# A new written-out order for the first batch, and the next batch's product of keys one step later

## The chip, the cores and the metric

The kernel runs on one core of one Trainium2 chip. The metric is the device time of one launch in microseconds (us). A core has five engines that work side by side, each through its own instructions in the order in which they were written for it: TensorE (PE, matrix products; PEld is its weight load), VectorE (DVE), ScalarE (ACT), GpSimd (POOL) and SyncE (SP, here the queue that issues the DMA transfers). An instruction waits until what it reads is there and what it overwrites is free, and everything behind it on its engine waits with it.

## The reference

Three layers stand one behind the other. The weights of the second, `w_in` and `w_out`, come as 64-bit floats, which the kernel reads as pairs of 32-bit words.

```python
# attention: q, k, v [8, 8, 576, 64], phi [8, 8, 576, 32]
a = softmax(phi, axis=2)                       # over the 576 positions
k_m = einsum('bhsm,bhsd->bhmd', a, k)          # product of keys
v_m = einsum('bhsm,bhsd->bhmd', a, v)          # product of values
x = softmax(q @ k_m.T / 8) @ v_m               # [8, 8, 576, 64] -> 4608 x 512
# a layer with ELU: w_in 512 x 2048, w_out 2048 x 512 (64-bit floats)
h = x @ w_in
y = where(h > 0, h, exp(min(h, 0)) - 1) @ w_out
# one of eight experts per row: w1 512 x 1024, w2 1024 x 512
e = argmax(y @ w_gate); out = gate * relu(y @ w1[e]) @ w2[e]
```

## The kernel before, in words

**Steps.** A batch is 576 rows, taken as two groups `g` of 288 columns; the ELU layer's 2048 inner columns are 16 blocks `f`. One step `(b, g, f)` is `mm1` (6 matmuls on PE, L509), `elu` (ACT L516, L517, DVE L518), `split_g` (`gh`, ACT's cast L525, and the rest `gl = e - gh`, L526, on DVE or POOL) and `mm2` (12 matmuls, L541: for each of four accumulators `gh`, `gl`, and `gh` with the low part `wol` of the weights). Each fp32 product is split into a high and a low part in this way. There are 256 steps; the first 25, of batch 0 (its second group is begun first, 8 blocks, then the first group), have numbers in the order below (`mm1.23`, `g.23`).

**Conversion.** In the first batch the weights are also loaded and converted, as 16 slices `n` of 1024 KB (even: `w_in`, odd: `w_out`). `x.n` loads one (SP, L241 or L249), `A0.n` is on ACT (L264, L269), `A1.n` three instructions on DVE (L278, L281, L284), `R.n` one on POOL (L292). Four slices (`FINE`) are done in two halves. For `w_in` the slice is then multiplied with the values (`M.s` PE L471, `Me.s` ACT L480 and DVE L481) and written out (`B.n`); for `w_out` it is cast (`C.n`, ACT L308) and its low part formed (`D.n.u`, L320: 4 of the 16 on PE, 5 on DVE by `LO_V`, 7 on POOL). The sixteenth slice's `D.15.0` and `D.15.1` are the last, and step 23 (`mm2.23`, block 15) needs them.

**Attention.** For a batch and each half `u` of the heads: loads `phi.u` (288 KB), `kv.u` (2 x 576 KB), `q.u` (three pieces, 576 KB); `a1` to `a2` the first softmax; `a3` the product of keys and values (PE L369), `a3b` (DVE L379 to L388); `a4t` turns the queries over (DVE L400), `a4` the scores (PE L413); `a5` (DVE L423), `a5e` (POOL L428), `a5b`, `a5m` (POOL L441), `a5c` (DVE L446), `a5d` (ACT L458, POOL L459). A name with `n.` in front belongs to the next batch (1), whose attention is prepared in the first batch's last steps. Its keys and values go into the buffer in which the slices were converted (tag `kv`, one buffer), its queries into one of two buffers that slices also use (tag `big`). `w.k` loads a converted part of `w_in` again; `n.M.k` multiplies it with batch 1's values. `routing` sets the tables for the third layer up (POOL, a few small DVE casts, and a DMA that fills `itab`).

**Order.** `START` is a list of these names; the program calls them in that order, and so sets each engine's order by hand, up to step 23. `LATER` gives the names that come at the head of steps 24 and on. From step 24 a scheduler places the instructions. `GL_V` lists the steps among the first 25 whose `gl` is formed on DVE; the others' are formed on POOL.

Of the kernel before, what the change touches and what calls it, by code (L numbers as in the profile page):

```python
# [23 lines left out]


START = """
routing phi.0 R.2.1 A1.9.1 x.1 kv.0 a1.0 A1.2.1 phi.1 a1e.0 A0.1 a2.0.0 R.7.1 a2.0.1 A1.1.0 A1.1.1 R.1.1 R.1.0 a3.0
q.0 a1.1 a1e.1 a2.1.0 a3b.0 A1.8.1 R.5.1 a4t.0 x.2 kv.1 a2.1.1 A0.2 a4.0 C.1 q.1 a5.0 R.3.1 A1.7.1 x.3 A1.2.0 x.0
a5e.0 a5b.0 D.1.1 D.1.0 a5m.0 a4t.1 a3.1 R.2.0 x.5 a5c.0 a3b.1 a4.1 a5d.0 A1.3.1 a5.1 A0.3 A1.3.0 a3c A0.0 a5e.1
a5b.1 M.1 A1.0.0 R.3.0 R.0.1 A0.5 a5m.1 a5c.1 x.4 C.3 D.3.0 R.11.1 R.0.0 Me.1 A0.4 x.6 a5d.1 D.3.1 A1.4.0 B.2 M.0  # L30
Me.0 R.4.1 A1.5.0 mm1.0 A0.6 elu.0 mm1.2 A1.6.0 R.14.1 elu.2 R.4.0 g.0 A1.4.1 M.2 Me.2 mm1.1 R.5.0 elu.1 R.12.1 C.5
mm1.3 A1.6.1 B.4 elu.3 D.5.1 g.1 mm1.4 R.6.0 R.8.1 g.2 x.7 mm2.0 A0.7 A1.5.1 R.6.1 M.3 A1.7.0 elu.4 mm1.5 A1.15.1
D.5.0 A1.14.1 x.8 mm2.1 x.9 mm2.2 g.3 Me.3 elu.5 mm1.6 mm1.7 B.6 mm2.3 R.7.0 A0.8 g.4 elu.6 A1.8.0 mm1.8 A1.12.1
A1.11.1 elu.7 C.7 mm2.4 g.5 A0.9 mm1.9 g.7 g.6 A1.9.0 D.7.1 R.8.0 B.0 x.10 elu.8 D.7.0 B.8 A1.0.1 R.9.0 elu.9 A0.10
mm2.5 g.8 swap R.9.1 mm2.6 n.phi.0 A1.10.0 mm1.10 mm2.7 M.4 elu.10 R.15.1 C.9 g.9 x.11 x.12 part mm1.11 elu.11
R.10.0 mm1.12 mm2.8 A1.10.1 Me.4 mm1.13 mm2.9 elu.12 g.10 A0.11 D.9.0 D.9.1 A1.11.0 mm1.15 R.10.1 x.13 mm2.10 elu.13
M.5 mm1.14 g.11 g.12 mm2.11 A0.12 A1.12.0 mm2.12 R.11.0 g.13 B.10 mm2.13 elu.14 Me.5 elu.15 C.11 n.a1.0 g.14 R.12.0
D.11.0 mm1.17 A0.13 D.11.1 M.6 mm1.16 elu.17 mm2.14 A1.13.0 x.14 mm1.18 g.15 elu.16 g.17 mm2.15 A1.13.1 R.13.0 Me.6
elu.18 g.16 A0.14 mm1.19 A1.14.0 R.13.1 mm2.16 g.18 elu.19 B.12 x.15 A0.15 n.q.0 mm1.20 A1.15.0 R.14.0 C.13 mm2.17
mm2.18 g.19 w.0 elu.20 M.7 Me.7 mm1.21 elu.21 D.13.0 g.20 mm2.19 g.21 R.15.0 C.15 mm1.22 n.phi.1 D.13.1 mm2.20  # L40
D.15.1 elu.22 D.15.0 B.14 mm2.21 g.22 n.q.1 n.kv.0 n.a4t.0 n.a1e.0 w.1 mm2.22 n.a2.0 n.a1.1 mm1.24 mm1.23 n.a4t.1
elu.24 elu.23 g.24 g.23 n.a1e.1
"""
# [1239 lines left out]
```

## Time and profile before

| | us |
|---|---|
| median of 3 runs | 1393.47 |
| lowest and highest of them | 1391.57, 1393.93 |
| the profiled execution | 1395.19 |
| its span in the profile | 1393.5 |

The profile is that of one execution; its times count from the span's start. A wait stands in brackets behind the instruction that waited, with what released it. The page's busy shares are means over the whole span; the change touches its first seventh.

### The profile page before, as it was taken

To read this page: it belongs to the slowest core of one execution; us is meant where nothing else is said; L and a number is where in the kernel's file an instruction comes from. 1 tells how busy PE (TensorE), PEld (TensorE's weight loads), DVE (VectorE), ACT (ScalarE), POOL (GpSimd) and SP (SyncE) were. 2 spreads that over 40 slices of the span, in tenths; PEclk is the share of its full clock that TensorE was granted. 3 is DMA by queue.
4 is the path that set the end of the run, shared out by engine and by line. 5 is a ranking of instruction groups with operands and counts; after the bars stand their busy time and mean duration, and the time that the engine had idled before them with its cause. 6 is when DMAs were issued, how large, how long until landed. Compare 5 with 4: busy or idle time off the path is not lost. (4 is left out here: it accounts for less than half of the span.)

```text
span 1393.5 us, 27587 instructions
## 1 busy us (share of the span) xinstructions
PE 1299.6 (93%) x9407; PEld 1114.5 (80%) x9407; DVE 626.4 (45%) x1359; ACT 633.6 (45%) x1377; POOL 433.9 (31%) x476
## 2 busy tenths in 40 slices
PE   4497899999999999999999999999999999999996
PEld 2287688889889889799789899878888888888885
DVE  4899564434534434444443324654223555342221
ACT  3577455555555555555555646423112344231110
POOL 2555143433433434334344343221111111111111
PEclk9999999999999999999999999999999999999998
DMA  9766656324434433442521510063111444111010
GB/s 211 198 192 198 171 140 133 90 90 97 106 80 98 136 71 94 112 94 75 130 48 42 163 33 18 18 222 129 38 46 42 167 149 144 60 47 47 32 47 31
DMA packets 57626, 140.74 MB, mean 101 GB/s; under 512 B 9321, under 2 KB 21738, under 8 KB 53872
## 3 DMA queue, kind: packets, MB, share of 16 engines
q1 hardware_dynamic: 49328, 118.15, 31.4%
q0 software_dynamic: 8128, 20.50, 4.6%
q8 instruction: 85, 1.39, 0.5%
q14 instruction: 85, 0.70, 0.2%
HBM read 253.79 MB, written 24.02 MB: 199 GB/s over the span
## 5 line engine op out<-in xcount | busy, mean ns | idle before, releaser
L541 PE MATMUL ps_acc<-gl,wt 128*128 128x288 f32 x1024 | 305.7, 299 | 6.4 <-DVE gl L526 3.7
L526 POOL TENSOR_TENSOR gl<-e,gh 128x288 fp32r<-128x288 f32 x237 | 192.0, 812 | 382.2 <-ACT gh L525 296.7
L541 PE MATMUL ps_acc<-gh,wt 128*128 128x288 f32 x1024 | 304.4, 297 | 0.0
L541 PE MATMUL ps_acc<-gh,wol 128*128 128x288 f32 x1024 | 302.2, 295 | 0.0
L509 PE MATMUL ps_h<-ath,wt 128*128 128x288 f32 x1024 | 261.9, 311 | 16.4 <-DVE e L518 15.9
L509 PEld LDWEIGHTS ps_h<-ath,wt 128*128 128x128 f32 x1024 | 179.5, 189 | 58.2 <-issue 29.9
L518 DVE SCALAR_TENSOR_TENSOR e<-e,ps_h 128x288 f32<-128x288 f32 x256 | 115.1, 450 | 230.1 <-ACT e L517 200.7
L541 PEld LDWEIGHTS ps_acc<-gl,wt 128*128 128x128 f32 x1024 | 194.6, 190 | 11.3 <-POOL gl L526 5.6
L1109 PE MATMUL ps_h<-wt,xh 128*128 x592 | 195.1, 400 | 1.3 <-ACT xh L1090 0.8
L541 PEld LDWEIGHTS ps_acc<-gh,wt 128*128 128x128 f32 x1024 | 194.9, 190 | 0.6 <-issue 0.6
L541 PEld LDWEIGHTS ps_acc<-gh,wol 128*128 128x128 f32 x1024 | 194.3, 190 | 0.0
L525 ACT CAST gh<-e 128x288 fp32r<-128x288 f32 x256 | 109.9, 430 | 152.3 <-DVE e L518 150.4
L1150 POOL DMA_INDIRECT out_dram<-ot,idw x37 | 37.1, 1004 | 388.4 <-DVE ot L1149 376.6
L509 PE MATMUL ps_h<-atl,wt 128*128 128x288 f32 x512 | 152.4, 298 | 0.0
L516 ACT ACTIVATE e<-ps_h 128x288 f32<-128x288 f32 x256 | 105.0, 410 | 89.0 <-PE ps_h L509 71.4
L1109 PEld LDWEIGHTS ps_h<-wt,xh 128*128 128x128 f32 x592 | 111.4, 188 | 27.0 <-ACT xh L1090 1.0
L1143 PE MATMUL ps_acc<-wt1h,hh 128*128 x296 | 120.6, 407 | 5.6 <-PEq L1187 5.6
L1125 ACT CAST hh<-ps_acc 128x512 fp32r<-128x512 f32 x74 | 39.8, 590 | 175.6 <-PE ps_acc L1123 175.5
L1143 PE MATMUL ps_acc<-wt1l,hh 128*128 x296 | 118.4, 400 | 0.0
L1143 PE MATMUL ps_acc<-wt1h,hl 128*128 x296 | 117.7, 397 | 0.0
L1109 PE MATMUL ps_h<-wt,xl 128*128 x296 | 117.2, 396 | 0.2 <-DVE xl L1091 0.2
L517 ACT ACTIVATE e<-e 128x288 f32<-128x288 f32 x256 | 113.8, 444 | 7.2
(242 smaller groups left out, 1824.9 us busy)
## 6 DMA issues: line engine op xcount, KB each, us to landing
raw<-in_moe_w_dram SPq DMA_DIRECT2D x78, 2048.0 KB
win<-win_s SPq DMA_DIRECT2D x28, 1024.0 KB
kv<-in_k_dram SPq DMA_DIRECT2D x16, 576.0 KB
kv<-in_v_dram SPq DMA_DIRECT2D x16, 576.0 KB
table<-yr SPq DMA_DIRECT2D x144, 64.0 KB
big<-in_moe_w_out_dram SPq DMA_DIRECT2D x10, 512.0 KB
phi_t<-in_phi_dram SPq DMA_DIRECT2D x16, 288.0 KB
big<-in_q_dram SPq DMA_DIRECT2D x16, 288.0 KB
```

The source lines that it names most:

```text
L509: nc.tensor.matmul(ps, x[:, u, fo:fo + P], y[:, u], start=(n == 0), stop=(n == 3 * NQ - 1))
L516: nc.scalar.activation(out=e, in_=ps, func=AF.Relu, scale=-1.0)
L517: nc.scalar.activation(out=e, in_=e, func=AF.Exp, scale=-1.0)
L518: nc.vector.scalar_tensor_tensor(out=e, in0=e, scalar=-1.0, in1=ps, op0=ALU.add, op1=ALU.max)
L525: nc.scalar.copy(out=gh, in_=e)
L526: eng.tensor_tensor(out=gl, in0=e, in1=gh.bitcast(F32), op=ALU.subtract)
L541: nc.tensor.matmul(acc[c], x[:, f, P * c:P * c + P], y, start=(first and n == 0), stop=(final and n == 2),)
L1109: nc.tensor.matmul(ps, x[:, c], half(wt[0][y][2 * c + hf]), start=(i == 0), stop=(i == 3 * NC - 1))
L1125: nc.scalar.copy(out=h, in_=ps)
L1143: nc.tensor.matmul(ps, get(h, f), half(wt[1][y][f]), start=(i == 0), stop=(i == 3 * NF2 - 1))
L1150: nc.gpsimd.indirect_dma_start(out=out, out_offset=IndirectOffsetOnAxis(ap=at, axis=0), in_=ot, in_offset=None, bounds_check=NT - 1, oob_i ...
```

## The change

It writes another order for the first batch (`START`), moves one of the five `D` on DVE to another half (`LO_V`), forms five more `gl` of the first 25 on POOL (`GL_V` falls from 19 to 14), and sets the next batch's product of keys and what follows from it one step later (`LATER`).

```diff
--- before.py
+++ after.py
@@ -24,30 +24,30 @@
 START = """
-routing phi.0 R.2.1 A1.9.1 x.1 kv.0 a1.0 A1.2.1 phi.1 a1e.0 A0.1 a2.0.0 R.7.1 a2.0.1 A1.1.0 A1.1.1 R.1.1 R.1.0 a3.0
...
+R.2.1 phi.0 a1.0 kv.0 R.12.1 phi.1 a1e.0 R.5.1 A1.12.1 q.0 q.1 a2.0.0 a1.1 a2.0.1 R.3.1 a3.0 a3b.0 A1.8.1 kv.1 R.8.1
...
 """
 LATER = {
-    24: "n.a3.0 n.a3b.0 n.kv.1 n.a2.1",
-    25: "n.a4.0 n.a5.0 n.a5e.0",
-    26: "n.a3.1 n.a3b.1 n.a5b.0 n.a5m.0 n.q2.0",
-    27: "n.pk2 n.a3c n.a4.1 n.a5.1 n.a5e.1 n.a5c.0",
-    28: "n.M.0 n.a5b.1 n.a5m.1 n.q2.1",
-    29: "n.a5d.0 n.a5c.1 n.a5d.1",
+    25: "n.a3.0 n.a3b.0 n.kv.1 n.a2.1",
+    26: "n.a4.0 n.a5.0 n.a5e.0",
+    27: "n.a3.1 n.a3b.1 n.a5b.0 n.a5m.0 n.q2.0",
+    28: "n.pk2 n.a3c n.a4.1 n.a5.1 n.a5e.1 n.a5c.0 n.M.0",
+    29: "n.a5b.1 n.a5m.1 n.q2.1 n.a5d.0",
+    30: "n.a5c.1 n.a5d.1",
     31: "n.M.1",
     34: "n.M.2",
     38: "n.M.3",
@@ -171,9 +171,9 @@
             FINE = (1, 6, 10, 13)
             CUT_AT, START_AT = 8, 23
 
-            LO_V = {(3, 0), (5, 1), (13, 1), (15, 0), (15, 1)}
+            LO_V = {(3, 0), (5, 1), (13, 0), (13, 1), (15, 0)}
 
-            GL_V = {0, 1, 2, 4, 5, 6, 7, 8, 10, 11, 12, 14, 17, 19, 20, 21, 22, 23, 24}
+            GL_V = {0, 3, 5, 6, 7, 8, 14, 15, 16, 20, 21, 22, 23, 24}
             LO_PE = {(1, 0), (1, 1), (3, 1), (7, 0)}
```

**The first loads on SP.** Before, behind the load of `w_gate`, `itab` and `phi.0` are followed by slice x.1 (L249, two pieces) and only then by the keys and values (L196):

```order
L780 DMA itab<-nobody 128x288 [waits Pool_49]
L190 DMA phi_t<-in_phi_dram 128x576
L249 DMA win_x<-in_moe_w_out_dram 128x1024 x2
L196 DMA kv<-in_k_dram 96x4x384
L196 DMA kv<-in_v_dram 96x4x384
L190 DMA phi_t<-in_phi_dram 128x576 [waits DMAHW2_49,DVE_49]
L214 DMA big<-in_q_dram 128x576 [waits DMAHW0_49]
```

After, `phi.0` is followed by the keys and values, `phi.1` and both halves of the queries (L214):

```order
L190 DMA phi_t<-in_phi_dram 128x576
L196 DMA kv<-in_k_dram 96x4x384
L196 DMA kv<-in_v_dram 96x4x384
L190 DMA phi_t<-in_phi_dram 128x576 [waits DMAHW1_49,DVE_49]
L214 DMA big<-in_q_dram 128x576
L214 DMA big<-in_q_dram 96x576
L214 DMA big<-in_q_dram 32x576
L214 DMA big<-in_q_dram 128x576 [waits DMAHW0_49]
```

The attention's loads have moved ahead of all slices; `itab` has left the place.

**The last loads on SP before the scheduler's part.** Before, the second half of the next batch's queries, then the first half of its keys and values, then w.1; the first half of the queries and w.0 were issued earlier and stand further up:

```order
L214 DMA big<-in_q_dram 128x576 [waits DMAHW4_49,DMAHW5_49,Activation_49,Pool_49]
L214 DMA big<-in_q_dram 96x576
L214 DMA big<-in_q_dram 32x576 [waits DMAHW6_49]
L196 DMA kv<-in_k_dram 96x4x384 [waits DMAHW3_49,DVE_49,DMAHW7_49,PE_49,Activation_49]
L196 DMA kv<-in_v_dram 96x4x384 [waits DMAHW0_49]
L329 DMA win<-win_s 128x2048 [waits DMAHW1_49]
```

After:

```order
L196 DMA kv<-in_k_dram 96x4x384 [waits DMAHW1_49,DVE_49,DMAHW2_49,PE_49,Pool_49]
L196 DMA kv<-in_v_dram 96x4x384 [waits DMAHW3_49]
L214 DMA big<-in_q_dram 128x576 [waits DMAHW4_49]
L214 DMA big<-in_q_dram 96x576 [waits DMAHW5_49]
L214 DMA big<-in_q_dram 32x576 [waits DMAHW6_49]
L780 DMA itab<-nobody 128x288 [waits DMAHW7_49,Pool_49]
L329 DMA win<-win_s 128x2048 [waits DMAHW0_49]
```

Now the first half of the next batch's keys and values comes first, its queries' first half (the three L214 rows) behind it, and then `itab`, w.0 and w.1.

**The end of DVE's written order.** Before (big_1319 is the second half of the next batch's queries, gl_1383 and gl_1387 are the `gl` of steps 24 and 23, ysb takes the finished accumulators):

```order
L400 STREAM_TRANSPOSE big_1319<-big_1319 128x1152 [waits DMAHW6_49,DMAHW5_49,DMAHW4_49]
L380 RECIPROCAL rs_1328<-rs_1328 128x1 [waits DVE_49]
L518 SCALAR_TENSOR_TENSOR e_1374<-e_1374,ps_h_1359 128x288 [waits Activation_49]
L518 SCALAR_TENSOR_TENSOR e_1378<-e_1378,ps_h_1366 128x288 [waits Activation_49]
L526 TENSOR_TENSOR gl_1383<-e_1374,gh_1382 128x288 [waits PE_49,Activation_49]
L526 TENSOR_TENSOR gl_1387<-e_1378,gh_1386 128x288 [waits PE_49,Activation_49]
```

After (big_1357 is the first half of the next batch's queries, gl_1385 and gl_1390 are the `gl` of steps 24 and 23):

```order
L379 TENSOR_SCALAR rs_1382<-rs_1382 128x1 [waits Activation_49]
L147 COPY run_75<-ecap_71 128x8 [waits DVE_49]
L380 RECIPROCAL rs_1382<-rs_1382 128x1 [waits DVE_49]
L526 TENSOR_TENSOR gl_1385<-e_1327,gh_1384 128x288 [waits PE_49,Activation_49]
L400 STREAM_TRANSPOSE big_1357<-big_1357 128x1152 [waits DMAHW6_49,DMAHW5_49,DMAHW4_49]
L526 TENSOR_TENSOR gl_1390<-e_1353,gh_1389 128x288 [waits PE_49,Activation_49]
L558 COPY ysb_1405<-ps_acc1_859 128x288 [waits PE_49]
```

A transpose that waits for the three pieces of `n.q.0` now stands between the last two subtractions; before, both transposes stood ahead of the two `elu`.

**PE around the product of keys.** Before, the last matmul of mm1.23, then `n.a3.0` (L369, waits for the two pieces of keys and values) ahead of and among the matmuls of mm2.23:

```order
L509 MATMUL ps_h_1366<-ath_356,wt0_79 128x288
L369 MATMUL ps_kv_1426<-kv_1323,a_1344 32x128 [waits DMAHW7_49,DMAHW0_49,Activation_49]
L541 MATMUL ps_acc0_858<-gh_1386,wt0_79 128x288 [waits Activation_49]
L369 MATMUL ps_kv_1426<-kv_1323,a_1344 32x128 x4
L541 MATMUL ps_acc0_858<-gl_1387,wt0_79 128x288 [waits DVE_49]
L541 MATMUL ps_acc0_858<-gh_1386,wol_114 128x288
```

After, mm2.23 follows mm1.23 directly; gl_1390 is the last subtraction of the rows above, and D.15.1 is on POOL; `n.a3.0` comes only behind mm2.24:

```order
L509 MATMUL ps_h_1342<-ath_276,wt0_79 128x288
L541 MATMUL ps_acc0_858<-gh_1389,wt0_79 128x288 [waits Activation_49]
L541 MATMUL ps_acc0_858<-gl_1390,wt0_79 128x288 [waits DVE_49]
L541 MATMUL ps_acc0_858<-gh_1389,wol_114 128x288 [waits Pool_49]
L541 MATMUL ps_acc1_859<-gh_1389,wt0_79 128x288
```

The first wait behind mm1.23 was one for keys and values, and is now one for `gh`, `gl` (DVE) and `wol` (POOL).

## Rows read from the trace of the kernel before

**Rows 1.** the page's part 1: busy time of each engine, instructions

```profile
PE 1299.6 (93%) x9407; PEld 1114.5 (80%) x9407; DVE 626.4 (45%) x1359; ACT 633.6 (45%) x1377; POOL 433.9 (31%) x476
```

**Rows 2.** stretches: PE, PEld, DVE, ACT, POOL, clock, DMA share, GB/s

```profile
10.00:20.00 10.00, 3.90 (x54) 3.02 (x52) 4.89 (x11) 2.86 (x7) 2.51 (x2) 1.00 1.08 214
...
140.00:150.00 10.00, 4.92 (x39) 4.68 (x37) 6.84 (x14) 5.46 (x13) 0.00 (x0) 0.90 0.92 235
```

**Rows 3.** timeline of SP's queue: start, us, DMA issue

```profile
1.56 0.45 SPq L128 DMA_DIRECT2D wg<-in_moe_w_gate_dram  x1
...
3.46 0.37 SPq L780 DMA_DIRECT2D itab<-nobody  x1
...
140.49 0.33 SPq L196 DMA_DIRECT2D kv<-in_k_dram  x1
```

**Rows 4.** timeline of PE: start, us, instruction, wait before it

```profile
17.10 2.79 PE L369 MATMUL ps_kv<-kv,a 96*32 96x128 f32 x48 [5.99 <-DMA kv<-in_v_dram]
...
32.41 2.79 PE L369 MATMUL ps_kv<-kv,a 96*32 96x128 f32 x48
...
59.95 0.40 PE L509 MATMUL ps_h<-ath,wt 128*128 128x288 f32 x1 [0.52 <-ACT wt L480]
...
144.63 0.29 PE L509 MATMUL ps_h<-ath,wt 128*128 128x288 f32 x1
...
150.64 0.60 PE L369 MATMUL ps_kv<-kv,a 96*32 96x128 f32 x2 [5.72 <-DMA kv<-in_v_dram]
...
180.78 0.40 PE L602 MATMUL ps_r<-r_oh,ones 96*128 96x24 f32 x2 [2.06 <-DVE wt L481]
...
185.79 0.29 PE L509 MATMUL ps_h<-ath,wt 128*128 128x288 f32 x1
```

**Rows 5.** timeline of ACT: slice x.4 has landed

```profile
52.32 1.14 ACT L264 ACTIVATE conv_h<-big 128x1024 f32<-128x1024 f32 x1 [0.16 <-DMA big<-in_moe_w_in_dram]
```

**Rows 6.** timeline of DVE: conversion, attention and transpose

```profile
28.95 0.69 DVE L281 TENSOR_SCALAR t<-t 128x1024 uint32<-128x1024 uint32 x1
...
29.68 1.23 DVE L284 SCALAR_TENSOR_TENSOR t<-win_x,t 128x1024 uint32<-128x1024 uint32 x1
...
41.21 0.75 DVE L423 TENSOR_REDUCE mx<-sT 128x18 f32<-128x576 f32 x1
...
48.25 0.63 DVE L278 TENSOR_SCALAR t<-t 128x1024 f32<-128x1024 f32 x1
...
129.03 2.76 DVE L278 TENSOR_SCALAR conv_h<-conv_h 128x1024 f32<-128x1024 f32 x1
...
140.64 1.38 DVE L400 STREAM_TRANSPOSE big<-big 128x1152 f32<-128x1152 f32 x1
...
180.08 1.25 DVE L481 TENSOR_TENSOR wt<-ps_M,wt 128x512 fp32r<-128x512 f32 x2
```

**Rows 7.** timeline of POOL: attention's instructions and two conversions

```profile
27.21 1.16 POOL L428 TENSOR_TENSOR sT<-sT,mx 128x576 f32<-128x576 f32 x1 [10.61 <-DVE mx L423]
...
32.23 1.16 POOL L441 TENSOR_TENSOR sT<-sT,sm 128x576 f32<-128x576 f32 x1 [3.86 <-DVE sm L436]
...
36.98 1.55 POOL L459 TENSOR_TENSOR atl<-atT,ath 128x288 fp32r<-128x288 f32 x2 [1.25 <-ACT ath L458]
...
128.82 2.40 POOL L292 TENSOR_TENSOR conv_h<-conv_h,win_x 128x1024 uint32<-128x1024 uint32 x1 [1.90 <-DMA big<-in_q_dram]
...
180.69 1.56 POOL L459 TENSOR_TENSOR atl<-atT,ath 128x288 fp32r<-128x288 f32 x2 [1.35 <-ACT ath L458]
```

**Rows 8.** single lines: count, ns least/median/most, first and last start

```profile
L526 DVE TENSOR_TENSOR gl<-e,gh x17: 444/1185/2669, 68.0 to 140.3; 128x288 fp32r<-128x288 f32 x17
...
L526 POOL TENSOR_TENSOR gl<-e,gh x237: 790/808/1023, 77.0 to 878.3; 128x288 fp32r<-128x288 f32 x119
...
L320 DVE TENSOR_TENSOR wol<-conv_h,wt x5: 677/684/2410, 52.3 to 139.7; 128x512 fp32r<-128x512 f32 x5
...
L320 POOL TENSOR_TENSOR wol<-conv_h,wt x7: 1296/1479/1748, 73.5 to 131.2; 128x512 fp32r<-128x512 f32 x7
```

More of the change, by code (lines that the diff above doesn't have):

```diff
@@ L26 @@
 START = """
-routing phi.0 R.2.1 A1.9.1 x.1 kv.0 a1.0 A1.2.1 phi.1 a1e.0 A0.1 a2.0.0 R.7.1 a2.0.1 A1.1.0 A1.1.1 R.1.1 R.1.0 a3.0
[L28 to L41, printed above, removed]
@@ L42 @@
-elu.24 elu.23 g.24 g.23 n.a1e.1
+R.2.1 phi.0 a1.0 kv.0 R.12.1 phi.1 a1e.0 R.5.1 A1.12.1 q.0 q.1 a2.0.0 a1.1 a2.0.1 R.3.1 a3.0 a3b.0 A1.8.1 kv.1 R.8.1
+a1e.1 a4t.0 a2.1.0 a2.1.1 a4.0 x.2 x.3 a5.0 a5e.0 A1.7.1 x.0 a4t.1 a5b.0 R.0.1 a5m.0 a5c.0 a3.1 a5d.0 a3b.1 a4.1
+A1.0.1 A0.2 a5.1 A1.5.1 A0.3 a3c a5e.1 A1.2.0 x.1 A0.0 A1.3.0 a5b.1 R.2.0 A1.0.0 M.1 Me.1 A1.2.1 R.3.0 C.3 R.9.1
+A0.1 a5m.1 R.0.0 a5c.1 A1.1.0 R.4.1 A1.1.1 x.4 a5d.1 D.3.1 M.0 R.7.1 x.5 A0.4 A1.4.0 Me.0 A1.4.1 mm1.2 D.3.0 A1.3.1
+elu.2 R.1.0 R.1.1 x.6 A0.5 mm1.1 A1.5.0 C.1 R.4.0 B.2 g.2 elu.1 M.2 Me.2 mm1.0 A0.6 R.5.0 x.7 C.5 A1.6.0 mm1.3 elu.0
@@ new lines @@
+D.1.0 g.0 A1.6.1 B.4 R.6.0 elu.3 g.1 D.5.1 D.1.1 A0.7 mm1.4 A1.7.0 mm2.0 R.6.1 mm1.5 D.5.0 M.3 mm2.1 mm2.2 R.7.0 x.8
+elu.4 elu.5 Me.3 A0.8 g.3 A1.8.0 mm1.6 mm1.7 mm2.3 B.6 g.4 mm2.4 x.9 C.7 elu.6 g.5 elu.7 mm1.9 A0.9 elu.9 g.6
+A1.15.1 g.7 D.7.0 D.7.1 A1.9.0 mm1.8 elu.8 mm1.10 mm2.5 mm2.6 n.phi.0 x.10 B.0 elu.10 x.11 mm1.11 R.8.0 A0.10
+A1.10.0 M.4 A1.9.1 A1.14.1 R.9.0 mm2.7 g.8 g.9 swap C.9 mm1.12 R.10.0 elu.11 part elu.12 D.9.1 B.8 mm1.14 A1.10.1
+x.12 D.9.0 mm2.8 g.10 mm2.9 R.11.1 R.10.1 Me.4 mm1.13 A0.11 M.5 R.14.1 mm2.10 g.11 x.13 A1.11.0 elu.14 g.12 elu.13
@@ new lines @@
+Me.5 R.11.0 mm2.11 n.a1.0 A0.12 B.10 A1.12.0 x.14 mm1.15 elu.15 g.13 mm2.12 mm1.16 mm2.13 g.14 C.11 mm1.17 A0.13
+A1.13.0 elu.16 R.12.0 g.15 mm2.14 elu.17 M.6 mm1.18 A1.13.1 D.11.1 R.15.1 g.16 mm2.15 mm1.19 D.11.0 B.12 Me.6 elu.18
+A0.14 x.15 mm2.16 R.13.0 mm1.20 n.phi.1 R.13.1 A1.14.0 A1.11.1 g.17 g.18 elu.19 A0.15 A1.15.0 elu.20 mm2.17 mm1.21
+R.14.0 mm2.18 g.19 C.13 M.7 mm2.19 Me.7 mm1.24 elu.21 D.13.0 mm1.22 g.20 R.15.0 D.13.1 C.15 g.21 mm2.20 n.q.1 D.15.0
+elu.22 g.22 mm2.21 mm2.22 B.14 n.a4t.1 n.a1e.0 D.15.1 n.kv.0 elu.24 n.a2.0 mm1.23 n.a1.1 elu.23 n.q.0 routing w.0
@@ L43 @@
+w.1 n.a1e.1 g.24 n.a4t.0 g.23
 """
 LATER = {
-    24: "n.a3.0 n.a3b.0 n.kv.1 n.a2.1",
-    25: "n.a4.0 n.a5.0 n.a5e.0",
-    26: "n.a3.1 n.a3b.1 n.a5b.0 n.a5m.0 n.q2.0",
-    27: "n.pk2 n.a3c n.a4.1 n.a5.1 n.a5e.1 n.a5c.0",
-    28: "n.M.0 n.a5b.1 n.a5m.1 n.q2.1",
-    29: "n.a5d.0 n.a5c.1 n.a5d.1",
+    25: "n.a3.0 n.a3b.0 n.kv.1 n.a2.1",
[4 more added lines that the diff above has]
+    30: "n.a5c.1 n.a5d.1",
```

## The prediction, made before the change was run

> **What bounds the kernel now.** First the page's busy shares: PE is busy for 1299.6 us of the span of 1393.5, 93% [rows 1]. Its idle time lies mostly ahead of the first `mm1`, at 59.95 us [rows 4], and in two waits of the next batch's attention: 5.72 us for keys and values at 150.64, 2.06 us at 180.78 [rows 4]. Behind these PE is nearly full, so what the start gains or loses by 186 us passes to the end, one to one. The question is what sets the start's end.
>
> Second, the stretches of 10 us. Between 10 and 20 us the DMA engines are full, at 214 GB/s [rows 2]: the start is bound by loads. Between 140 and 150 us PE is busy for 4.92 us only [rows 2]: the wait for the keys.
>
> Third, who ends last. The keys' load is issued at 140.49 [rows 3], because its buffer is the one in which the slices are converted; the conversion's last instruction frees it. I call this moment K (140.5). PE ends mm1.23 at 144.9 and resumes at 150.64 [rows 4], that is K + 10.1. So K and what follows it set the time, and PE's own work ahead of K does not.
>
> Fourth, what sets K. The conversion's DVE and POOL instructions do not run side by side. An L278 takes 0.63 us with POOL idle (48.25) and 2.76 at 129.03 [rows 6], where POOL runs an L292 of 2.40 from 128.82 [rows 7]. The `gl` subtractions on DVE take 0.444 us at least and 1.185 in the median, the most 2.669 [rows 8]. So I count both engines' work with two SBUF inputs or in this fast form as one queue, each at its unstretched duration. One slice is 0.63 + 0.69 + 1.23 on DVE [rows 6] and 2.40 on POOL [rows 7]: 4.95 us. From 40 to 140.4 us it holds 14 of the 16 slices (69.3), five `D` on DVE at 0.68 and seven on POOL at 1.30 (12.5), 17 `gl` on DVE at 0.444 and six on POOL at 0.808 (12.4) [rows 8], and the second half's attention on POOL, 1.16 + 1.16 + 1.55 (3.9) [rows 7]. That is 98.1 of 100.4 us: the pair of engines is full at a pace of 0.977, and K is when this queue is empty.
>
> The Trainium skill, page "SBUF — State Buffer", section "SBUF: two separate sides", says that VectorE and GpSimd share one port pair as an exclusive lock, taken for a whole instruction. The 2.76 us beside the 2.40 agree with it. By this rule the five `gl` that leave DVE cost time, where by DVE's busy time they would give 5.9 us back; that second reading is rival 1.
>
> **The change part by part.**
>
> *Loads.* Before, 7,712 KB landed between a3.0 at 17.10 [rows 4] and slice x.4 at 52.32 [rows 5]: phi.1, q.0, x.2, kv.1, q.1 and four slices, 219 KB per us. a3.0 waited for 2,608 KB (itab, phi.0, x.1, kv.0), 11.9 us, so the flow began at 5.2, 1.7 behind the issue of itab at 3.46 [rows 3]. Now phi.0 follows `w_gate`, whose issue ends at 2.0 [rows 3]: the flow begins at 3.8. kv.0 (1,440 KB in) lands at 10.4, kv.1 (4,032 KB) at 22.2, x.2 at 26.9, then a slice every 4.7 us. So a3.0 comes 6.7 us earlier, but no slice is there before 26.9, where before x.1 was converted ahead of the attention.
>
> *First conversion.* On DVE the first `A1` now stands behind a5.1's reduction. That came 9.5 us behind a3.1 before (32.41 [rows 4] to 41.96 [rows 6]); less what q.1's later landing had cost, 8.6 is my estimate. From 22.4 it ends at 31.0 (29.9 to 32.1). Attention comes 6 to 10 us earlier and the first `mm1` perhaps 8, but PE does not set K.
>
> *The queue of DVE and POOL.* Whole start before: 16 slices 79.2, `D` 12.5, `gl` 12.4, attention twice 3.9: 111.9 us. Five `gl` move to POOL: 5 x (0.808 - 0.444) [rows 8] = 1.8, so 113.7. D.15.1 moves to POOL and D.13.0 to DVE: nothing. Until 31.0 only attention's first 3.9 can be done; 109.8 remain, with slices arriving every 4.7 us against 4.95 of work each, so the queue stays fed. At 0.977 that is 112.4 us, K = 143.4: **+2.9**. Lower bound: never idle, 140.8, +0.3. Upper: from 32.1 at a pace of 0.96, +6. I take +3.
>
> *The wait at the end.* n.a3.0 stands behind mm2.24 now, so the 5.72 us for keys end. But mm2.23's second matmul needs g.23, which DVE does only behind n.a4t.0, and that waits for n.q.0, issued behind n.kv.0 and so at K + 1 at the earliest. What lay hidden ahead of both `elu` is now on the path. Neither the order's effect on a load of queries nor this wait is in the trace of before; the nearest row is the keys' own, usable at K + 10.1 with w.1 beside them. I let n.q.0 land then too, and add the transpose, 1.38 [rows 6], the subtraction, 0.45 [rows 8], and 0.15 between engines: K + 12.1, **+2.0** against K + 10.1. Lower bound: only kv and q, 1,728 KB at the 235 GB/s of that stretch [rows 2], 7.4 us, and 0.5 + 1.9: K + 9.8, -0.3. Upper: itab and half of w.0 and w.1 get in between, 2,896 KB, 12.3 us, and 1.9: K + 14.2, +4.1. PE gets there at about 148 and waits some 7 us.
>
> *Later steps.* n.M.0's evacuation, for whose L481 at 180.08 [rows 6] PE waited 2.06 us at 180.78 [rows 4], now stands ahead of L446 on DVE: -2.06. The attention chain has one step less to mm1(32) at 185.79 [rows 4]: 18 matmuls, 2.4 us, against a slack of 3.5 behind POOL's 180.69 + 1.56 [rows 7]; other `gl` on POOL may eat that, +1. Together **-1** (-3 to +1). w.0, itab and routing are later but not needed for 20 us; their cover is n.kv.0's own wait. The five `gl` on POOL delay PE nowhere near K.
>
> Sum: +3 + 2 - 1 = **+4**. The profiled execution took 1395.19 us, 1.7 above the median of 1393.47; from it 1399.2, from the median 1397.5.
>
> **The rivals.** What this kernel's measurement can tell from no change is about 0.2%, 2.8 us.
>
> 1. *Faster: DVE's own queue sets K.* If the stretched durations were DVE's own and POOL free, five `gl` at the median of 1.185 us [rows 8] would leave it: -5.9, and +1.0 for the late first slice; with +2 and -1 the sum is -3.9, **1389.6**. For it: that median is far above the least, whatever stretches it. Against: the same L278 at 0.63 and 2.76, and the sum of 98.1 in 100.4. It decides from K before 139.5, where the sum changes its sign, and counts as faster from 136.7. Chance 0.22.
>
> 2. *Same.* The queue never idles from 31.0 (K + 0.3) and the queries land early (-0.3 to +2): -1 to +1.5, **1394**. For it: slices stand ready from 27 us. Against: the pace was not 1.0 before. Chance 0.25.
>
> 3. *Much slower.* K + 5 and n.q.0 last of a crowd (+4), -1: +8, **1401.5**. For it: itab, w.0 and w.1 follow directly on SP. Chance 0.12, part of the slower half.
>
> 4. *The key wait is truly gone*, because n.q.0 lands before PE reaches mm2.23: -5.7 + 3 - 1 = -3.7, 1389.8. It would need 1,728 KB in 4.4 us, 390 GB/s where 235 was seen. Chance 0.03; with rival 1 faster has 0.25.
>
> **How the numbers follow.** The forecast, +2.8 to +6.5, has 0.38 and with rival 3 slower has 0.50; same 0.25; faster 0.25. The range leaves out a tenth at each end: from 1389.5, just under rivals 1 and 4, to 1401.5, rival 3. The likeliest case alone spans 1396 to 1400.
>
> **What would show it.** a3.0 at 10 to 11 us and the first `mm1` near 52; the first whole L278 only at 30 to 32; n.kv.0's issue at 143 to 144; behind mm1.23 a wait of PE for DVE's L526, with L400 waiting for the queries just ahead, until K + 12; no wait of L369 for keys; the wait at L602 gone or small. I am wrong if n.kv.0 is issued before 140 (then the queue is not what sets K), or if PE passes mm2.23 without a wait of several us.

## The result: 1.1% slower, half of it lost in one wait behind a scatter

The change makes the kernel slower: a median of 1406.90 us (1404.73 to 1408.80, 6 runs) against 1392.33 (1390.26 to 1393.93, 6 runs) for the kernel before, a ratio of 1.0112 with a 95% interval of 1.0097 to 1.0127. Forecast were 1397.5 and a range up to 1401.5: the direction was right, and the size is outside the range. The profiled execution took 1408.80 us, its span is 1407.0. One of the ten executions of the kernel e9 below took 1819.65 us at a mean granted clock of 0.661, in a slow state that no other execution here shows, and is left out of that kernel's figures.

The signs that the prediction named come first. The page's part 1 of the kernel after (busy time, instructions) answers to [rows 1]; PE has the same instructions and is 6.3 us longer busy:

```profile
PE 1305.9 (93%) x9407; PEld 1119.2 (80%) x9407; DVE 633.6 (45%) x1354; ACT 632.8 (45%) x1377; POOL 440.5 (31%) x481
```

SP's timeline of the kernel after (start, us, DMA issue), for [rows 3]:

```profile
2.60 0.43 SPq L196 DMA_DIRECT2D kv<-in_k_dram  x1
...
141.24 0.33 SPq L196 DMA_DIRECT2D kv<-in_k_dram  x1
...
143.11 1.58 SPq L214 DMA_DIRECT2D big<-in_q_dram  x3
...
192.20 0.36 SPq L190 DMA_DIRECT2D phi_t<-in_phi_dram  x1
192.65 0.37 SPq L329 DMA_DIRECT2D win<-win_s  x1
```

K, the issue of the next batch's keys, is 141.24 (140.49 before). The queries follow at 143.11. The last two rows come into play further down.

PE's timeline of the kernel after, for [rows 4] (in brackets the wait before the instruction and what released it):

```profile
11.61 2.79 PE L369 MATMUL ps_kv<-kv,a 96*32 96x128 f32 x48 [1.93 <-DMA kv<-in_v_dram]
...
51.58 0.61 PE L509 MATMUL ps_h<-ath,wt 128*128 128x288 f32 x1
...
148.25 0.61 PE L541 MATMUL ps_acc<-gh,wt 128*128 128x288 f32 x1 [2.61 <-ACT gh L525]
153.50 0.61 PE L541 MATMUL ps_acc<-gl,wt 128*128 128x288 f32 x1 [4.65 <-DVE gl L526]
...
161.31 0.96 PE L369 MATMUL ps_kv<-kv,a 96*32 96x128 f32 x26
...
183.11 0.40 PE L602 MATMUL ps_r<-r_oh,ones 96*128 96x24 f32 x2 [0.67 <-DVE wt L481]
...
204.03 0.61 PE L509 MATMUL ps_h<-ath,wt 128*128 128x288 f32 x1 [4.70 <-DVE e L518]
...
205.63 0.44 PE L541 MATMUL ps_acc<-gh,wt 128*128 128x288 f32 x1
205.87 0.44 PE L541 MATMUL ps_acc<-gl,wt 128*128 128x288 f32 x1
```

Down to 183.11 this is what was forecast: `a3.0` at 11.61 (17.10 before), the first `mm1` at 51.58 (59.95), no wait for keys at 161.31, and in its place waits for `gh` and `gl` that end at 153.50, K + 12.3. PE's wait at L602 falls from 2.06 us to 0.67. There PE is 2.3 us behind the kernel before (183.11 against 180.78), and 2.6 at the L564 near 196 us. The row at 204.03 was not forecast: PE waits 4.70 us for `elu`, and from there its matmuls start 0.24 us apart instead of 0.13.

DVE's timeline of the kernel after, for [rows 6]:

```profile
32.45 0.68 DVE L278 TENSOR_SCALAR t<-t 128x1024 f32<-128x1024 f32 x1
...
151.73 1.38 DVE L400 STREAM_TRANSPOSE big<-big 128x1152 f32<-128x1152 f32 x1 [3.38 <-DMA big<-in_q_dram]
153.03 0.42 DVE L526 TENSOR_TENSOR gl<-e,gh 128x288 fp32r<-128x288 f32 x1
...
191.39 0.78 DVE L336 STREAM_TRANSPOSE pT<-phi_t 128x576 f32<-128x576 f32 x1 [0.80 <-POOL atl L459]
...
202.04 0.78 DVE L336 STREAM_TRANSPOSE pT<-phi_t 128x576 f32<-128x576 f32 x1 [6.10 <-DMA phi_t<-in_phi_dram]
...
203.53 0.81 DVE L518 SCALAR_TENSOR_TENSOR e<-e,ps_h 128x288 f32<-128x288 f32 x2
```

Rows two and three are the wait that was forecast: the transpose of the late queries, then step 23's `gl`. The last two are the one that was not: at 202.04 a transpose of batch 2's `phi` (L336, in `a1`) has waited 6.10 us for its load, and the two `elu` (L518) for which PE waits stand behind it.

### Where the wait at 202 us comes from

POOL's timeline of the kernel after, for the last row of [rows 7]. L665 is an indirect DMA that POOL issues: it scatters the numbers of 96 rows, 4 bytes each, into the experts' lists `itab`; three of them belong to batch 0's first group.

```profile
184.55 1.16 POOL L441 TENSOR_TENSOR sT<-sT,sm 128x576 f32<-128x576 f32 x1 [3.59 <-DVE r_f L631]
...
188.20 0.82 POOL L459 TENSOR_TENSOR atl<-atT,ath 128x288 fp32r<-128x288 f32 x1
189.41 1.11 POOL L665 DMA_INDIRECT itab<-ids,di  x1 [0.40 <-DVE r_f L636]
190.55 0.81 POOL L459 TENSOR_TENSOR atl<-atT,ath 128x288 fp32r<-128x288 f32 x1
191.52 0.93 POOL L665 DMA_INDIRECT itab<-ids,di  x1 [0.17 <-issue]
192.75 0.92 POOL L665 DMA_INDIRECT itab<-ids,di  x1 [0.30 <-issue]
```

The chain reads backwards. The load of `phi` for the second half of batch 2 is issued at 192.20, as soon as the single `phi` buffer is free, which L336 of the first half frees (it runs from 191.39 to 192.17). That L336 waits for L459 on POOL, because its result `pT` (L335) and attention's `atT` (L445) share one buffer (tag `pT`), and L459 reads `atT` last, at 190.55. So `n.a5d.1`, the last piece of the next batch's attention, sets when the next `phi` can be loaded. Before, its L459 stood at 180.69 [rows 7], the load was issued at 184.12 and the first L665 came at 186.93, 2.8 us behind it. From SP's and POOL's timelines of the kernel before (the first row takes in the next load of `phi`, at 191.23):

```profile
184.12 7.46 SPq L190 DMA_DIRECT2D phi_t<-in_phi_dram  x2
...
186.93 1.14 POOL L665 DMA_INDIRECT itab<-ids,di  x1 [0.82 <-DVE r_pos L637]
```

Now `n.a5d.1` stands one step later, among the ranking for the third layer: the L441 ahead of it (`n.a5m.1`) comes at 184.55 (178.18 before), and one of its two L459 stands behind the first scatter. The load is issued 2.8 us behind the first L665 instead of 2.8 ahead.

What the scatter does to a load shows in the stretches of 4 us (PE, PEld, DVE, ACT, POOL busy; granted clock; DMA share; GB/s). The DMA share adds up the durations of the packets, as a part of 16 engines' time, and can exceed 1. The kernel after:

```profile
192.00:196.00 4.00, 2.58 (x25) 2.16 (x17) 3.94 (x10) 2.85 (x7) 2.18 (x3) 1.00 0.83 32
196.00:200.00 4.00, 3.33 (x31) 2.65 (x29) 0.00 (x0) 2.09 (x5) 0.00 (x0) 1.00 0.92 41
200.00:204.00 4.00, 0.00 (x0) 0.00 (x0) 1.96 (x5) 0.00 (x0) 0.00 (x0) 0.85 0.78 300
204.00:208.00 4.00, 3.97 (x16) 3.98 (x17) 2.91 (x10) 2.78 (x7) 1.72 (x3) 0.50 1.30 60
```

The kernel before:

```profile
192.00:196.00 4.00, 3.93 (x34) 3.06 (x33) 1.96 (x4) 2.99 (x8) 0.80 (x1) 1.00 1.21 43
196.00:200.00 4.00, 4.00 (x43) 3.12 (x40) 1.75 (x10) 2.53 (x6) 1.13 (x2) 1.00 0.60 109
200.00:204.00 4.00, 4.00 (x38) 3.74 (x31) 2.51 (x8) 2.74 (x6) 1.24 (x2) 1.00 0.95 347
```

In both, the DMA engines count as busy behind the scatter (0.83 to 1.21) and move 32 to 43 GB/s, in the kernel before for one stretch and in the kernel after for two; 300 and more follow only from 200. Before, the load that somebody needed had left already and PE stayed full; now it lies in this hole. PE then does nothing for all of 200 to 204, and in 204 to 208 its granted clock is 0.50, the level of 1.2 GHz. 4.70 us of wait, 18 matmuls at 0.11 us more each (2.0) and L471 behind them (1.54 us instead of 1.09) are 7.1 of the 7.3 us that PE loses on what the kernel before does between 196 and 208: L654 comes at 218.44 there, and at 208.49 before, 9.95 later.

### The profile page after: what moved, and what is told of

The parts are those of the page before. It is cut to its first block, busy times and chain, and to the rows that moved or that the text cites. A ratio compares the mean times of both kernels' runs of the same rounds, so it can differ in the third digit from the quotient of the medians.

```text
span 1407.0 us, 27600 instructions
## 1 busy us (share of the span) xinstructions
PE 1305.9 (93%) x9407; PEld 1119.2 (80%) x9407; DVE 633.6 (45%) x1354; ACT 632.8 (45%) x1377; POOL 440.5 (31%) x481
## 5 line engine op out<-in xcount | busy, mean ns | idle before, releaser
L526 POOL TENSOR_TENSOR gl<-e,gh 128x288 fp32r<-128x288 f32 x242 | 197.5, 818 | 387.3 <-ACT gh L525 299.8
L541 PE MATMUL ps_acc<-gl,wt 128*128 128x288 f32 x1024 | 306.4, 299 | 9.7 <-DVE gl L526 7.4
L541 PE MATMUL ps_acc<-gh,wt 128*128 128x288 f32 x1024 | 304.7, 298 | 2.6 <-ACT gh L525 2.6
L541 PE MATMUL ps_acc<-gh,wol 128*128 128x288 f32 x1024 | 303.8, 297 | 0.0
L518 DVE SCALAR_TENSOR_TENSOR e<-e,ps_h 128x288 f32<-128x288 f32 x256 | 114.8, 450 | 230.5 <-ACT e L517 188.1
L541 PEld LDWEIGHTS ps_acc<-gl,wt 128*128 128x128 f32 x1024 | 194.4, 190 | 14.5 <-DVE gl L526 9.1
L541 PEld LDWEIGHTS ps_acc<-gh,wt 128*128 128x128 f32 x1024 | 194.7, 190 | 4.5 <-ACT gh L525 2.8
L541 PEld LDWEIGHTS ps_acc<-gh,wol 128*128 128x128 f32 x1024 | 194.6, 190 | 0.0
```

What stands on the lines that cost most here:

```text
L541: nc.tensor.matmul(acc[c], x[:, f, P * c:P * c + P], y, start=(first and n == 0), stop=(final and n == 2),)
```

## The experiments

Each kernel is compared with the kernel before on the same chip; the latter's median was 1392.51, 1396.08 and 1393.39 us in the three groups of runs, so ratios are compared, and what was expected in microseconds is read as a ratio too. The ratios are estimated from the executions themselves and differ from the quotients of the medians by about 0.001.

| kernel | median us | ratio (95%) |
|---|---|---|
| e1_later_old | 1400.80 | 1.0062 (1.0038 to 1.0086) |
| e2_later_new | 1395.53 | 1.0035 (1.0012 to 1.0059) |
| e3_phi_buffer | 1406.23 | 1.0107 (1.0071 to 1.0143) |
| e4_q0_first | 1401.15 | 1.0064 (1.0037 to 1.0090) |
| e5_q0_two_phi | 1395.83 | 1.0005 (0.9986 to 1.0024) |
| e6_later_two_phi | 1392.53 | 0.9971 (0.9952 to 0.9990) |
| e7_gl_pool | 1404.52 | one run |
| e8_scatter_late | 1408.81 | one run |
| e9_no_scatter_after | 1396.03 | 1.0010 (0.9991 to 1.0029) |
| e10_no_scatter_before | 1389.24 | 0.9972 (0.9948 to 0.9995) |
| e11_before_again | 1398.13 | one run |

Shifts of PE below are those of the same instruction against the profile of the kernel before.

### The two halves of the change

**e1_later_old**: the kernel after with the old `LATER`.

```diff
 LATER = {
-    25: "n.a3.0 n.a3b.0 n.kv.1 n.a2.1",
+    24: "n.a3.0 n.a3b.0 n.kv.1 n.a2.1",
...
-    30: "n.a5c.1 n.a5d.1",
+    29: "n.a5d.0 n.a5c.1 n.a5d.1",
```

> The changed kernel with the LATER table of before (the product of keys one step earlier again); the new START, GL_V and LO_V stay. Theory 1: of the 14.6 us that the change lost, about 7.3 come at 196 to 208 us, where VectorE waits 6.10 us for phi of batch 2, second half: its load is issued at 192.20, behind the first scatter of the third layer at 189.41, since the chain that ends in n.a5d.1 now ends one step later. With LATER back the load is issued before the scatter and the 7.3 us go; at mm2.23 the wait for gl or for the keys stays, so 1397 to 1400 us, PE's step at 208 us about 2 to 4 later than before. Theory 2 (rival): the loss belongs to the new START (five gl on GpSimd, late queries) and shows only later: 1404 us or more.

Measured: 1.0062 (1397 to 1400 of 1392.51 is 1.0032 to 1.0054), a little above what was expected. The load of `phi` is issued at 187.18, ahead of the first scatter at 189.61, and L336 does not wait. PE is 1.5 us late at 208, but at 231.62 DVE's L400 waits 3.41 us for batch 2's queries, issued behind the three scatters of batch 0's second group, and at 244 PE is 5.0 late. So the new `LATER` makes the wait at 202. The later wait can't be put down to the new order: the kernel before, run once more (e11), shows 3.15 us of it.

**e2_later_new**: the kernel before with the new `LATER` (the same lines, the other way round, on the old `START`).

> The kernel before with the LATER table of the change alone. Theory 1: at mm2.23 PE no longer waits 5.72 us for keys, since mm2.23, mm1.25, the logits, mm1.26 and mm2.24 (about 5 us) come first: -4 to -5; then phi of batch 2 falls behind the scatter and VectorE waits 6 us: +7.3. Sum +2.5 to +3.5: 1395 to 1396 us. Theory 2: only the gain, 1387 to 1389 us.

Measured: 1.0035. DVE's timeline of this kernel, two transposes of `phi`:

```profile
182.07 0.78 DVE L336 STREAM_TRANSPOSE pT<-phi_t 128x576 f32<-128x576 f32 x1 [0.79 <-POOL atl L459]
...
193.08 0.78 DVE L336 STREAM_TRANSPOSE pT<-phi_t 128x576 f32<-128x576 f32 x1 [6.45 <-DMA phi_t<-in_phi_dram]
```

PE stands 6.7 us ahead of the kernel before at 193, and 1.2 behind it at 208: the step put later makes the same wait in the old order too, and eats all that it had won. Of the 6.7 us, 3.6 are not the table's: K is 136.93 in this profile and 140.49 in that of the kernel before, with the same order up to there (e11).

### Taking the load out of the scatter's way

**e3_phi_buffer**: the kernel after with a buffer of its own for this one `phi`, so that nothing holds its load back (it then goes out with the first loads, 288 KB more at the start).

```diff
-                t = pool.tile([P, NJ * M], F32, tag="phi", name="phi_t")
+                t = pool.tile([P, NJ * M], F32, tag="phi2" if (b, u) == (2, 1) else "phi", name="phi_t")
```

> The changed kernel with a buffer of its own for phi of batch 2, second half, so that this load waits for nothing (the scheduler puts it at the very start, 288 KB more there, 1.3 us of transfer at 219 KB per us). No other order changes. Theory 1: VectorE's 6.10 us wait and the 7.3 us go, the start may lose up to 1.3: 1399.5 to 1401 us. Theory 2 (the wait for phi is only where a delay of something else shows): PE waits for another thing there, 1406 to 1408 us.

Measured: 1.0107, a miss. The wait at 202 is gone and PE is 2.7 us late at 208 instead of 9.95. But batch 2's queries (L214 at 223.56, behind scatters at 207.56 to 210.93) come too late: L400 waits 5.09 us at 234.51, and PE is 7.9 late at 254. A loss comes at the next loads in its place.

**e8_scatter_late**: the kernel after with the ranking and the three scatters of batch 0's first group four steps later.

```diff
-                t = [1, 2, 6, 7, 6, 8, 10] if b == 0 and g == 0 else [1, 2, 4, 5, 6, 8, 10]
+                t = [1, 2, 10, 11, 6, 8, 10] if b == 0 and g == 0 else [1, 2, 4, 5, 6, 8, 10]
```

> The changed kernel with the ranking and the scatter of batch 0's first group four steps later (step 33 and on); phi keeps its one buffer and is still freed at about 192 us. If the scatter delays the load: phi lands 3 us after its issue, VectorE waits under 1 us for it, and PE at 208 us is only 2.7 later than before instead of 9.9. If the load is slow for another reason (its place on the queue, the transfer of w behind it): it still takes 9 to 10 us.

Measured, SP's and DVE's timelines of this kernel:

```profile
190.15 0.35 SPq L190 DMA_DIRECT2D phi_t<-in_phi_dram  x1
...
193.11 0.78 DVE L336 STREAM_TRANSPOSE pT<-phi_t 128x576 f32<-128x576 f32 x1 [0.32 <-DMA phi_t<-in_phi_dram]
```

`phi` is issued with no scatter near it and is there 3.0 us later; PE is 2.8 late at 202 and 3.7 at 208. With six scatters from 201.09 to 212 L400 then waits 3.72 us at 234.56, and PE is 7.9 late at 244. Only the ranking and the scatters were moved, so with them ahead of it the load is late; e9 tells the scatters from the ranking. And again a loss comes further on.

**e9_no_scatter_after**: the kernel after without batch 0's six scatters (batch 0's rows are missing from the third layer's lists).

```diff
             def y_scatter(b, g, i):
+                if b == 0:
+                    return
                 t = (G // PK) * (2 * b + g) + i
```

> The changed kernel without the six scatters of batch 0 (L665, three for each group, 96 numbers of 4 bytes each): batch 0's rows are then missing from the third layer's lists; nothing else is left out, and no other instruction changes its place. If the scatters are what holds up the loads behind them: phi of batch 2, issued at 192.2, lands some 3 us later and not 9.8, VectorE's 6.1 us wait for it goes, and no load of batch 2 is late at 230 us: 1398 to 1400 us, 7 us faster than the change. If the loads are slow for another reason, 1406 to 1408.

Measured: 1.0010, better than expected. The stretches of this kernel:

```profile
188.00:192.00 4.00, 4.00 (x38) 3.00 (x38) 3.93 (x13) 2.27 (x5) 1.30 (x2) 1.00 0.27 76
192.00:196.00 4.00, 3.31 (x28) 2.45 (x27) 3.79 (x8) 3.54 (x9) 0.00 (x0) 1.00 0.82 278
196.00:200.00 4.00, 4.00 (x40) 3.74 (x46) 2.43 (x10) 2.88 (x8) 1.56 (x2) 1.00 0.59 159
```

The hole is gone: with nearly the DMA share of the kernel after (0.82 and 0.83), 278 GB/s move in 192 to 196 instead of 32, though w is issued close behind `phi` here too (191.06 and 189.85). The second half's L336 does not wait. The wait for `gl` is there as before (4.65 us, until 151.76, K + 12.1); PE is 0.6 late near 200 and 0.4 ahead at 244.

**e10_no_scatter_before**: the same edit on the kernel before.

> The kernel before without the six scatters of batch 0 (batch 0's rows are missing from the third layer's lists, nothing else). In before no instruction waited over 0.5 us for a load in the scatters' shadow, so by the same theory it gains nothing beyond the noise: ratio to before 0.998 to 1.001, and the changed kernel without scatters stands only 4 to 7 us above it, the part that is made at mm2.23.

Measured: 0.9972, slightly better than expected: the kernel before pays a little for the scatters too. The pair e9 and e10 is the change without scatters: 0.0038 of 1392 us, 5.3 us, known to some 4 by the two intervals (half-widths 0.0019 and 0.0024). The medians of the two, 1396.03 and 1389.24 from one group of runs, differ by 6.8. All of the change is 0.0112, 15.6 us, and 14.6 by its medians. So 8 to 10 us of it need the scatters.

### The start's own terms

**e7_gl_pool**: the kernel before with all of these `gl` on POOL, to tell the shared queue from DVE's own (rival 1).

```diff
-            GL_V = {0, 1, 2, 4, 5, 6, 7, 8, 10, 11, 12, 14, 17, 19, 20, 21, 22, 23, 24}
+            GL_V = set()
```

> The kernel before with GL_V empty: all 25 subtractions gl of the first batch on GpSimd, 17 of them ahead of K (the issue of the next batch's keys) taken from VectorE. If VectorE and GpSimd are one queue, as in my sum: K later by 17 x 0.364 = 6.2 us, 146 to 147. If VectorE's own queue set K: 17 x 1.185 = 20 us are taken from it and K is earlier by 5 us or more, 135 or less.

Measured: K = 146.97, by SP's timeline of this kernel, 6.48 us later than in the first profile of the kernel before:

```profile
146.97 0.33 SPq L196 DMA_DIRECT2D kv<-in_k_dram  x1
```

The single line L526 of this kernel, 40 to 147 us (count, ns least/median/most, first and last start), shows all of them on POOL:

```profile
L526 POOL TENSOR_TENSOR gl<-e,gh x23: 799/1004/1797, 63.7 to 146.8; 128x288 fp32r<-128x288 f32 x23
```

Taking 17 subtractions off DVE does not make K earlier, as rival 1 asked (135 or less), but later, so rival 1 falls. From 40 to 140 us DVE is busy for 87.1 us and POOL for 73.7 in this kernel, so neither is full by itself. The size is less sure than 6.48 beside 17 x (0.808 - 0.444) = 6.2 makes it look: K of the old order lies between 136.93 and 140.49 (e11), and against these this run is 6.5 to 10.0 later.

**e4_q0_first**: the kernel after with the halves of the next batch's queries exchanged, so that the transpose that waits stands behind step 23's `gl`.

```diff
-R.14.0 mm2.18 g.19 C.13 M.7 mm2.19 Me.7 mm1.24 elu.21 D.13.0 mm1.22 g.20 R.15.0 D.13.1 C.15 g.21 mm2.20 n.q.1 D.15.0
-elu.22 g.22 mm2.21 mm2.22 B.14 n.a4t.1 n.a1e.0 D.15.1 n.kv.0 elu.24 n.a2.0 mm1.23 n.a1.1 elu.23 n.q.0 routing w.0
-w.1 n.a1e.1 g.24 n.a4t.0 g.23
+R.14.0 mm2.18 g.19 C.13 M.7 mm2.19 Me.7 mm1.24 elu.21 D.13.0 mm1.22 g.20 R.15.0 D.13.1 C.15 g.21 mm2.20 n.q.0 D.15.0
+elu.22 g.22 mm2.21 mm2.22 B.14 n.a4t.0 n.a1e.0 D.15.1 n.kv.0 elu.24 n.a2.0 mm1.23 n.a1.1 elu.23 n.q.1 routing w.0
+w.1 n.a1e.1 g.24 g.23 n.a4t.1
```

> The changed kernel with the two halves of the next batch's queries exchanged (n.q.0 is loaded early, n.q.1 last) and the late transpose (now n.a4t.1) moved behind g.23 on VectorE. Takes the wait for gl at mm2.23 away. Theory 1: mm2.23 starts at about 148 us and not at 153.3; n.a3.0 then waits for keys until about 151.5, so at n.a3.0 PE is 4 to 5 us earlier and the scatter and phi move with it: 1402 to 1403 us. Rival: the time to the scatter is set by the chain from the keys (issued at 141.2 in both), so the gain is lost again by 208 us: 1406 to 1408 us.

Measured: 1.0064. PE's wait for `gl` is gone and `n.a3.0` comes 4.7 us earlier than in the kernel after; PE is 2.1 ahead of the kernel before at 193. Then L336 waits 5.86 us at 197.10 for the same `phi`, and PE is 4.5 behind at 208. So the forecast wait is real and can be mended, and the other is independent of it.

### Both mended

**e5_q0_two_phi**: e4 with two `phi` buffers (the gather that borrows this buffer takes two as well).

```diff
-                t = pool.tile([P, NJ * M], F32, tag="phi", name="phi_t")
+                t = pool.tile([P, NJ * M], F32, tag="phi", name="phi_t", bufs=2)
...
-                t = pool.tile([P, DM], F32, tag=("phi", "pT")[s], name="xe")
+                t = pool.tile([P, DM], F32, tag=("phi", "pT")[s], name="xe", bufs=2 - s)
```

> The changed kernel with both mends together: the queries' halves exchanged and the late transpose behind g.23 (as in the run before), and two buffers for phi, so that phi of batch 2, second half, is loaded long before the first scatter. Theory 1 (two separate losses, at mm2.23 and at the load in the scatter's shadow): VectorE's 5.9 us wait for phi is gone, PE at 208 us stands 2 us ahead of the kernel before and not 4.5 behind: 1392 to 1396 us, the upper end if the queries' load of batch 2 at about 230 us takes 3 to 5 us back, as it did in the two runs without the wait for phi. Rival (the chain of loads decides in any case): 1399 to 1402 us.

Measured: 1.0005, inside 1392 to 1396 (0.9996 to 1.0025 of 1392.51). PE is 1.6 ahead of the kernel before from 193 to 208, and then waits 4.41 us for keys at 228.89 while L400 waits 7.69 for queries at 233.73.

**e6_later_two_phi**: the kernel before with the new `LATER` and the two `phi` buffers (the lines of e2 and e5).

> The kernel before with the LATER table of the change and two buffers for phi; START, GL_V and LO_V of before. Theory 1: the 6.5 us wait of VectorE for phi is gone, and the 4 to 6 us stay that the later product of keys had won by 195 us: 1386 to 1390 us, faster than both kernels; up to 1393 if the queries' load of batch 2 at 230 us takes some back. Rival: 1395 us as with the table alone.

Measured: 0.9971, faster than both kernels, and as a ratio inside what was expected (1386 to 1390 of 1392.51 is 0.9953 to 0.9982). PE is 5.6 ahead at 209, 2.3 of it by an earlier K (138.20), and still pays further on: at 244 it is 3.5 behind in this profile. POOL's timeline of this kernel has the last of the second group's scatters:

```profile
201.74 0.92 POOL L665 DMA_INDIRECT itab<-ids,di  x1 [0.30 <-issue]
```

SP's timeline of this kernel has the issues of batch 2's keys and of its queries:

```profile
205.93 0.46 SPq L196 DMA_DIRECT2D kv<-in_k_dram  x1
...
221.92 0.37 SPq L214 DMA_DIRECT2D big<-in_q_dram  x1
```

PE's timeline of this kernel has the wait for the keys:

```profile
226.97 1.30 PE L369 MATMUL ps_kv<-kv,a 96*32 96x128 f32 x20 [6.29 <-DMA kv<-in_v_dram]
```

And DVE's timeline of this kernel has the wait for the queries:

```profile
231.66 1.38 DVE L400 STREAM_TRANSPOSE big<-big 128x1152 f32<-128x1152 f32 x1 [9.44 <-DMA big<-in_q_dram]
```

The keys, issued 4 us behind the last of the second group's scatters, are there only 21 us after their issue. (This profiled execution took 1398.13 us, where the median of the ten is 1392.53.)

**e11_before_again**: the kernel before, unchanged, once more.

> The kernel before once more, for how far K (the issue of the next batch's keys) moves from run to run: it was 140.49 in its first profile, and 136.93 and 138.20 in two kernels with the same START up to there. I expect 137 to 141; the five kernels with the new START had 140.3 to 141.2 (and 141.9 with 288 KB more at the start).

Measured: 1398.13 us, K = 139.66, and by DVE's timeline L400 waits 3.15 us for batch 2's queries, where the first profile shows 0.44:

```profile
227.21 1.38 DVE L400 STREAM_TRANSPOSE big<-big 128x1152 f32<-128x1152 f32 x1 [3.15 <-DMA big<-in_q_dram]
```

So this wait varies by 2.7 us, and K by 0.8, with one program; of the waits of L400 in e1, e3, e5, e6 and e8 (3.41 to 9.44 us), only what lies clearly above 3.15 can be due to an edit. It is gone in e9 and e10, without the scatters, but also in e2, where the scatters (206.05 to 208.50) and the queries behind them (222.42) are issued nearly as in e1 (206.28 to 208.73, 221.66). Of the kernels with the old `START` and the old `GL_V`, K was 140.49, 136.93, 138.20, 137.09 and 139.66 (mean 138.5); with the new ones 141.24, 140.28, 140.34, 140.80, 140.63 and 139.70 (mean 140.5; e3, with more to load, 141.93).

## Why the prediction was right and wrong, point by point

**The start, and K: the direction right, the term too large.** `a3.0` came at 11.61 (10 to 11 forecast), the first `mm1` at 51.58 (52), the first whole L278 at 32.45 (30 to 32). Forecast was K + 3, at 143 to 144; it came at 141.24. The two first profiles differ by 0.75, the means over the kernels by 2.0, inside the bounds of 0.3 and 6. That work moved from DVE to POOL makes K later is shown by e7; that it does so by the difference of the durations is borne out only within the 3.5 us by which K varies. One row was read loosely: POOL is not idle beside the L278 at 48.25, its L441 starts at 48.48 and takes 1.41 us, where the one in [rows 7] takes 1.16; there POOL is the one that is stretched. The line L526, 40 to 141 us, first on POOL in the kernel before, then in the kernel after, answers to [rows 8]:

```profile
L526 POOL TENSOR_TENSOR gl<-e,gh x6: 957/998/1023, 77.0 to 126.0; 128x288 fp32r<-128x288 f32 x6
```

```profile
L526 POOL TENSOR_TENSOR gl<-e,gh x11: 801/1170/1275, 61.9 to 131.8; 128x288 fp32r<-128x288 f32 x11
L526 DVE TENSOR_TENSOR gl<-e,gh x11: 446/459/2529, 69.9 to 138.8; 128x288 fp32r<-128x288 f32 x11
```

With more of them on POOL the median there is 1.170 us instead of 0.998, and on DVE 0.459 instead of 1.185: the stretch has moved from DVE towards POOL. (The 0.808 that the prediction took for POOL is the median over the whole kernel.) The Trainium skill, page "SBUF — State Buffer", section "SBUF: two separate sides", states the lock between these two engines, and e7 agrees with it in direction: 17 instructions moved from one to the other made K later and not earlier.

**The wait at the end: right.** L541 resumed at K + 12.3 in the kernel after, at K + 12.0 in e8 and K + 12.1 in e9 (12.1 forecast), behind L400's wait for the queries, as described; e4 takes the wait away by exchanging the halves. The keys' wait is gone.

**L602: right for the most part.** 2.06 us became 0.67. Up to 196 us PE is 2.6 us late, against the +4 of the sum; over the runs e9 and e10 the change without scatters costs 5.3 us by the ratios and 6.8 by the medians.

**"Later steps: together -1": this is the step that failed.** It followed the attention's chain to the matmul that needs it, mm1(32), found 2.4 us against a slack of 3.5, and let routing pass as "later but not needed for 20 us". It did not follow what the chain sets free. `n.a5d.1` frees the tile in which batch 2's `a1` works, this frees the one `phi` buffer, and that lets the next load go. None of these links is an instruction that PE waits for at once, and the load had a slack against L665 of 2.8 us only. PE went on 2.9 us later behind the wait at the end (153.50 against 150.64) and is 9.95 late by 208 us, so the term measured +7 instead of -1; 7.3 us are lost between 196 and 208 alone. The runs e1, e2, e8 and e9 show its three conditions: the step one later (e1, e2), the scatter ahead of the load (e8), the scatter at all (e9). A premise fell with it, that what the start gains or loses by 186 us passes to the end one to one: PE of e6 is 5.5 us ahead at 225 and 3.5 behind at 244, and that of e11, the unchanged kernel, goes from 3.6 ahead to 0.5 behind.

**The rivals.** Rival 1 fell with e7. Rival 3 had the sign, but its mechanism (queries last of a crowd) did not come: L541 kept to K + 12.3. None had the load behind the scatter, so none reached 1406.9.

**What stays open.** Between 208 us and the end the kernel after loses a further 3.6 us (9.95 at L654, 13.5 in the span): +2.7 near 690 us, +2.0 near 915, and some given back between. The first varies as much among the other profiles (-1.4 in e6, +4.2 in e11). The second stands in six of the seven profiles with the new `START` (1.9 to 2.3 us; e5 0.65) and is -0.1 to 1.5 us in the others; PE's granted clock is 0.66 there in the kernel after (926 to 931 us) and 1.00 in the kernel before (915 to 920). No run was made for either. Why K varies by 3.5 us under the old `START` is open too. And the split of the loss into 5 to 7 us without scatters and 8 to 10 with them rests on ratios with intervals of 0.002 each, so its parts are known to some 4 us. That the scatters of the second group make the queries late is not shown: without scatters no wait is left, but e2 has none with them either.

## What to carry to other kernels

When a chain moves by one step, follow not only who reads its results but which buffers it frees, through every tile that shares a tag, to the next load that this lets go; then see what else is on the DMA engines at the moment of that issue. A transfer of few bytes can be no small transfer: this scatter of 4-byte elements belongs behind the loads that are needed soon. And a mended load can show the next one: e3, e5 and e8 won the first wait and lost most of it again 30 us later, so only a profile to the end of the disturbed stretch tells what an edit is worth.
